# Gated mix of attention and a state-space convolution: the skip term as a lag-0 tap, five-chunk master blocks without negated copies, and zero-weight filler matmuls

## Chip, cores and metric

One NeuronCore of a Trainium2 chip. The metric is the device time of one execution in microseconds (us); the kernel before has a median of 537.9 us over 4 runs. All three parts of the change are in one kernel file, which builds its own instruction order by a planner in Python before anything runs.

## What is computed

x is 2048 x 448 (bf16). Two branches read it and a gate mixes them:

```python
g = sigmoid((x * gate_w).sum(-1, keepdims=True))
a = attention(x)          # 16 heads of 28, one shared k and v, softmax over 2048 keys, then @ wo
b = conv(x, K) + x * Dskip
out = g * a + (1 - g) * b
```

K is a causal kernel of 2048 lags for each of the 448 channels: `K[d, l] = Re sum_n C[d,n] * dB[d,n] * exp(l * dt[d] * A[d,n])` with 256 complex modes n. The reference convolves by FFT; the kernel does it by matmuls with a Toeplitz matrix.

## The kernel before, in words

**Order of work.** Every operation is recorded by `Prog.op` with an engine, a planned duration, the keys that it reads and writes, and a priority `pr` (lower goes first). `Prog.schedule` (L116) then goes through the operations as a list scheduler: of all that are ready, the one with the earliest planned start, then the lowest `pr`, goes next on its engine. It adds 107 ns (`SWITCH`) when the tiling mode of PE changes (`mode`: full, r32, c32, c64). The result is one fixed order per engine, and `emit` (L210) writes it out with semaphore waits. Each engine runs its list in order, so what stands behind a waiting instruction waits too.

**Attention.** 16 groups (4 blocks of 512 queries, 4 groups of 4 heads), each of 16 key tiles x 4 heads: 1024 score tiles of 128 keys x 512 queries. `qk` (L967) makes 3 or 2 of them at a time in one half of psS (two times three banks), as row-tiled matmuls (r32, 29 rows). ACT takes exp of 3 or 2 tiles in one instruction (L977) into a ring of 10 tiles. `pv` (L985) multiplies 4 tiles of one key tile by v with four column-tiled matmuls (c32) and accumulates in the bank psB over 16 key tiles. Then DVE copies the bank out (L933), and the division by the sums goes through small DMAs (L944). `outp` (L877, L883) multiplies by wo and adds the gated result into O (SBUF, all 2048 x 448 outputs). The last group has its own ending (`norm_last`, L899 to L920). `qproj` (L676 to L685) makes the queries of a group two groups ahead in bank psX.

**Convolution.** 28 chunks of 16 channels. Powers of the modes are built from "masters": `masters(b)` squares the complex step ten times (L717, L720, L723), for a block of 4 chunks at once, and writes each level's real part, imaginary part (L727) and negated imaginary part (L730) to mbf. mbf has two halves, used by alternate blocks. `tables(c)` starts from the seeds (L746) and doubles the table five times per chunk: product with the real part (L759), product with the imaginary part into tmp (L762), sum with swapped halves (L767); two more products make the last level (L776, L778). `kgen(c)` multiplies tables on PE (L792) to the 2048 lags of the chunk's kernel; DVE rounds them to kstg (L804, L807) and a DMA puts them into the scratch KP in HBM. `conv(c)`, two chunks later in the program, loads Toeplitz tiles of 1 MB (`tload`, ring of 4), multiplies them by the stored x (U) with four column-tiled matmuls each (L853), multiplies by 1 - g on DVE (L861), transposes on PE (L831) and adds into O (L838). A chunk's L838 touches rows of all four query blocks.

**The skip term.** At the end `skip` (L452) loads x and Dskip again into xT, which is free by then, and DVE does x * (1 - g) * Dskip (L462) and O + that (L465) for each of 16 row tiles, at `pr` 90. `store` then writes each of the four query blocks of O (two on SP's queue, two on ACT's), once all additions to it are done.

**Banks.** psX is shared by qproj, kgen, the transposes and outp under a lock; one bank of psS is shared by kernel preparation and conv.

Of the kernel before, what the change touches and what calls it, by code (L numbers as in the profile page):

```python
# [48 lines left out]
class Op:  # L49
    __slots__ = ("i", "eng", "fn", "ns", "lat", "deps", "pr", "lock", "unlock", "slot", "ndma",  # L50
                 "count", "vc", "end", "comm", "slack", "mode")


class Prog:
# [3 lines left out]
    SWITCH = 107.0  # L58

# [8 lines left out]
    def op(self, eng, fn, ns, rd=(), wr=(), pr=0, lat=60, lock=None, unlock=None, comm=(), slack=None, mode="full"):  # L68
# [5 lines left out]
        o.comm, o.mode = comm, mode  # L74
# [41 lines left out]
    def schedule(self):  # L116
# [18 lines left out]
        pemode = None  # L135
        done = 0
        while done < n:
# [37 lines left out]
            if o.slot is not None:  # L175
                free[e] = r + 450.0 * o.ndma
                s = max(r, dmafree)
                dmafree = s + o.ns
                end = dmafree + self.DMA_NS
            else:  # L180
                ns = o.ns
                if e == "pe":
                    if o.mode != pemode:
                        ns += self.SWITCH
                    pemode = o.mode
                free[e] = r + ns
                end = free[e] + o.lat
# [22 lines left out]
    def emit(self, block):  # L210
# [61 lines left out]
        for e in ENG:  # L272
# [3 lines left out]
            def body(x, e=e):  # L276
                for o, waits in lists[e]:
                    for s, v in waits.items():
# [17 lines left out]
class Kernel:  # L296
# [10 lines left out]
    def build(self):  # L307
        nc = self.nc
        with self.es:
            self.pg = Prog(nc, self.es)  # L310
            self.alloc()
# [13 lines left out]
    def alloc(self):  # L325
# [32 lines left out]
        sizes = [4] * 7  # L358
# [3 lines left out]
        self.AO = [0, 4, 128, 132, 256, 384]  # L362
        self.BO = [448 + 128 * k for k in range(6)]
        self.MC = 448 + 5 * 128 + 64
# [11 lines left out]
        self.zero = sb("zero", 2, BF)  # L376
# [5 lines left out]
    def consts(self):  # L382
# [11 lines left out]
        pg.op("dve", lambda e: e.memset(V(self.kstg, 0, 256), 0.0), 100, wr=[("kst", 0)])  # L394
        ms(self.Wk, NT * P, 0.0, "Wk")
# [15 lines left out]
    def loads(self):  # L411
# [32 lines left out]
        pg.op("dve", lambda e: e.tensor_copy(self.Wv.v(0, DT, 28, [[32, 4]]), self.smallb.v(0, DT, 0, [[1, 4]])), 80, rd=["smb"], wr=["Wv"])  # L444
        w = ins["A_wo"]
# [5 lines left out]

    def skip(self):  # L452
        pg, ins = self.pg, self.ins
        tab = self.xT
        keys = [("xT", hf, j) for hf in range(4) for j in range(2)]
        pg.dma([(tab.v(0, P, 0, [[D, 16], [1, D]]), dram(ins["A_x"], 0, [[D, P], [P * D, 16], [1, D]])),
                (tab.v(0, P, 16 * D, [[1, D]]), dram(ins["B_Dskip"], 0, [[0, P], [1, D]]))],
               (2176, 896), "xs", wr=["xs"] + keys, pr=4)
        for i in range(16):
            tv = tab.v(0, P, D * i, [[1, D]])  # L460
            ov = self.O.v(0, P, D * i, [[1, D]])
            pg.op("dve", lambda e, tv=tv, i=i: e.scalar_tensor_tensor(tv, tv, self.gtok.v(0, P, 16 + i, [[1, 1]]),  # L462
                                                                      tab.v(0, P, 16 * D, [[1, D]]), ALU.mult, ALU.mult),
                  el(D), rd=["gt", "xs"], wr=[("xg", i)], pr=90)
            pg.op("dve", lambda e, tv=tv, ov=ov: e.tensor_tensor(ov, ov, tv, ALU.add),  # L465
                  el(D, 1.92), rd=[("xg", i)], comm=[("O", i // 4)], pr=90)
# [221 lines left out]
    def masters(self, b):  # L688
# [5 lines left out]
        A0 = lambda lv: mo + (BC * (self.AO[lv] // 128 * 128) + self.AO[lv] % 128)  # L694
        pr = 51.5 + c0 if b else 1.4
# [12 lines left out]
        for k in range(11):  # L708
            ks = "sz" if k == 0 else ("ms", k % 2)
            lv, w8 = (k, 16) if k < 5 else (5, 8) if k == 5 else (k - 6, 16)  # L710
            ro, io = A0(lv), mo + BC * self.BO[lv]
            sp_, sn_ = io + 4, io
            if k > 5:
                ro, sp_, sn_ = ro + 8, io + 8, io + 12
            lk = ("mb", b % 2, k)
            if k:
# [10 lines left out]
            pg.op("dve", lambda e, k=k, ro=ro, sp_=sp_, w8=w8: e.tensor_copy(  # L727
                mbf.v(0, P, ro, [[sp_ - ro, 2], [w8, 8 * BC], [1, 4]]), src_both(k)),
                el(2 * BW, 1.92), rd=kk, wr=[lk], pr=pr)
            pg.op("dve", lambda e, k=k, sn_=sn_, w8=w8: e.tensor_scalar(  # L730
                mbf.v(0, P, sn_, [[w8, 8 * BC], [1, 4]]), src(k, 1), -1.0, None, ALU.mult),
                el(BW, 1.92), rd=kk, wr=[(lk, 1)], pr=pr)

    def tables(self, c):
# [14 lines left out]
        for lv in range(5):  # L749
            w = 1 << lv  # L750
            ra = mo + BC * (self.AO[lv] // 128 * 128) + self.AO[lv] % 128 + 128 * ci
            rb = mo + BC * self.BO[lv] + 128 * ci
            mk = [("mb", b % 2, lv), (("mb", b % 2, lv), 1), ("mb", b % 2, lv + 6), (("mb", b % 2, lv + 6), 1)]
            rk = [("tab", s, l) for l in range(lv + 1)]
# [6 lines left out]
                el(n, 1.92), rd=rk + mk, wr=[("tab", s, lv + 1)], pr=pr)  # L761
            pg.op("dve", lambda e, a=src, rb=rb, w=w: e.tensor_tensor(  # L762
                tmp.v(0, P, so, [[4 * w, 32], [1, 4 * w]]), a,
                mbf.v(0, P, rb, [[4, 32], [0, w], [1, 4]]), ALU.mult),
                el(n, 1.92), rd=rk + mk, wr=[("tmp", s)], pr=pr)
            t2 = tmp.v(0, P, so + 4 * w, [[8 * w, 16], [-4 * w, 2], [1, 4 * w]])
            pg.op("dve", lambda e, d=dst, t=t2: e.tensor_tensor(d, d, t, ALU.add), el(n, 1.92),  # L767
                  rd=[("tmp", s), ("tab", s, lv + 1)], wr=[("tab", s, lv + 1)], pr=pr)
        ra = mo + BC * self.AO[5] + 64 * ci
# [323 lines left out]
```

## Time and profile before

| | |
|---|---|
| median of 4 runs | 537.9 us (537.64 to 542.41) |
| the profiled execution, its own time | 537.64 us |
| its span in the trace | 535.9 us |
| mean granted TensorE clock | 0.928 |
| exp on ACT (L977), 410 instructions | 470.5 us busy |
| L759, L762, L767 on DVE, 140 each | 78.5, 78.5, 78.4 us busy |
| DMA | 138.16 MB, mean 258 GB/s |

The span runs from the first to the last instruction in the trace. "L977" is line 977 of the kernel before. "out<-in" names the tiles. A group's mean is the time of one instruction; neighbours on an engine overlap a little, so the busy time of a group is less than count times mean. "a <- b" in the waits says that a started when b had finished. PEld are the weight loads of PE. In the clock row each digit is a tenth of the full TensorE clock, for one of 40 equal slices of the span.

### The profile page before, as it was taken

To read this page: it belongs to the slowest core of one execution; us is meant where nothing else is said; L and a number is where in the kernel's file an instruction comes from. 1 tells how busy PE (TensorE), PEld (TensorE's weight loads), DVE (VectorE), ACT (ScalarE), POOL (GpSimd) and SP (SyncE) were. 2 spreads that over 40 slices of the span, in tenths; PEclk is the share of its full clock that TensorE was granted. 3 is DMA by queue.
4 is the path that set the end of the run, shared out by engine and by line. 5 is a ranking of instruction groups with operands and counts; after the bars stand their busy time and mean duration, and the time that the engine had idled before them with its cause. 6 is when DMAs were issued, how large, how long until landed. Compare 5 with 4: busy or idle time off the path is not lost.

```text
span 535.9 us, 18403 instructions
## 1 busy us (share of the span) xinstructions
PE 478.6 (89%) x8214; PEld 243.8 (45%) x8229; DVE 483.4 (90%) x1168; ACT 487.2 (91%) x428; POOL 4.9 (1%) x17
## 2 busy tenths in 40 slices
PE   6768877998999899999999989999999998998893
PEld 5421122454545344554555435544555543554452
DVE  3978899899999999999999999999999999999023
ACT  3598989999999999999999999999999999999960
POOL 3000000000000000000000000000000000000000
PEclk9855566899999999999999999999999999999997
DMA  9724526588888777878988896878877896799954
GB/s 234 156 66 121 154 87 260 165 299 331 284 320 293 262 275 223 278 261 334 313 317 307 286 325 226 279 242 296 323 273 263 315 368 240 198 359 305 347 187 137
DMA packets 42266, 138.16 MB, mean 258 GB/s; under 512 B 8168, under 2 KB 24476, under 8 KB 27852
## 3 DMA queue, kind: packets, MB, share of 16 engines
q1 hardware_dynamic: 40396, 135.71, 74.2%
q10 hardware_dynamic: 1792, 1.29, 0.9%
q8 instruction: 64, 1.05, 0.8%
q14 instruction: 14, 0.11, 0.1%
HBM read 133.01 MB, written 3.85 MB: 255 GB/s over the span
## 4 chain that ended last, share of the span: by engine, by line
PE 40%; DVE 29%; ACT 27%; DMA 1%; issue 1%; DVEq 0%
ACT expT L977 26%; PE psS L967 11%; PE psS L853 10%; PE psB L985 7%; PE psX L792 5%; DVE tab L759 4%; DVE tmp L762 4%; DVE tab L767 4%; DVE tab L776 2%; PE psX L676 2%; DVE msq L717 2%; DVE tab L778 1%; DVE cst L861 1%; PE psS L504 1%; DVE mbf L727 1%; PE psX L877 1%
## 5 line engine op out<-in xcount | busy, mean ns | idle before, releaser
L977 ACT ACTIVATE expT<-psS 128x1536 bf16<-128x1536 f32 (+1 forms) x410 | 470.5, 1257 | 17.0 <-PE psB L985 11.7
L967 PE MATMUL psS<-qT,kT 29*128 29x512 bf16 x1024 | 169.8, 410 | 33.3 <-ACT expT L977 29.2
L853 PE MATMUL psS<-T,U 128*32 128x128 bf16 (+7 forms) x3584 | 157.2, 303 | 1.5 <-issue 1.0
L853 PEld LDWEIGHTS psS<-T,U 128*32 128x32 bf16 (+7 forms) x3584 | 113.7, 152 | 33.2 <-issue 26.9
L985 PE MATMUL psB<-expT,vaug 128*32 128x512 bf16 x1024 | 108.2, 414 | 1.5 <-ACT gtok L643 1.4
L967 PEld LDWEIGHTS psS<-qT,kT 29*128 29x128 bf16 x1024 | 39.6, 92 | 125.4 <-ACT expT L977 95.3
L762 DVE TENSOR_TENSOR tmp<-tab,mbf 128x2048 bf16<-128x2048 bf16 (+4 forms) x140 | 78.5, 567 | 0.0
L759 DVE TENSOR_TENSOR tab<-tab,mbf 128x2048 bf16<-128x2048 bf16 (+4 forms) x140 | 78.5, 567 | 0.0
L767 DVE TENSOR_TENSOR tab<-tab,tmp 128x2048 bf16<-128x2048 bf16 (+4 forms) x140 | 78.4, 568 | 0.0
L985 PEld LDWEIGHTS psB<-expT,vaug 128*32 128x32 bf16 x1024 | 26.6, 94 | 63.8 <-issue 60.4
L792 PE MATMUL psX<-tab 128*32 128x96 bf16 x1792 | 54.4, 268 | 0.8 <-issue 0.8
L792 PEld LDWEIGHTS psX<-tab 128*32 128x32 bf16 x1792 | 40.7, 116 | 13.6 <-issue 8.0
L776 DVE TENSOR_TENSOR tab<-tab,mbf 128x2048 bf16<-128x2048 bf16 x28 | 34.2, 1220 | 0.0
L778 DVE TENSOR_TENSOR tab<-tab,mbf 128x2048 bf16<-128x2048 bf16 x28 | 34.1, 1216 | 0.0
L861 DVE TENSOR_TENSOR cst<-psS,omq 128x512 bf16<-128x512 f32 x28 | 19.1, 682 | 14.9 <-PE psS L853 14.7
L717 DVE TENSOR_TENSOR msq<-mst 128x256 f32<-128x256 f32 x63 | 26.4, 419 | 0.0
L676 PE MATMUL psX<-xT,Wq 112*128 112x512 bf16 x64 | 21.8, 438 | 0.3 <-DVE O L838 0.2
L727 DVE CAST mbf<-mst 128x256 bf16<-128x256 f32 x70 | 20.4, 291 | 0.1
L720 DVE TENSOR_TENSOR mst<-msq 128x128 f32<-128x128 f32 x70 | 20.0, 286 | 0.0
L723 DVE SCALAR_TENSOR_TENSOR mst<-mst 128x128 f32<-128x128 f32 x63 | 18.0, 286 | 0.0
L730 DVE TENSOR_SCALAR mbf<-mst 128x128 bf16<-128x128 f32 x70 | 15.5, 221 | 0.0
L804 DVE TENSOR_REDUCE kstg<-psX 128x128 bf16<-128x256 f32 x28 | 11.8, 422 | 3.8 <-PE psX L792 3.7
(112 smaller groups left out, 252.2 us busy)
## 6 DMA issues: line engine op xcount, KB each, us to landing
T<-KP_scratch SPq DMA_DIRECT2D x112, 1024.0 KB, 7.9
rdenB<-R_scratch SPq DMA_DIRECT2D x60, 64.0 KB, 3.8
U<-in_A_x_dram SPq DMA_DIRECT2D x3, 896.0 KB, 5.4
tab<-in_A_x_dram SPq DMA_DIRECT2D x4, 448.0 KB, 7.0
O<-Z_scratch SPq DMA_DIRECT2D x1, 1792.0 KB, 13.4
KP_scratch<-kstg SPq DMA_DIRECT2D x28, 64.0 KB
xT<-in_A_x_dram SPq DMA_DIRECT2D x1, 1792.0 KB, 9.7
U<-Z_scratch SPq DMA_DIRECT2D x1, 896.0 KB, 7.9
```

The lines of the kernel that those rows point to most:

```text
L676: pg.op("pe", lambda e, T=T: e.matmul(px, self.Wq.v(0, DT, T * 512 + g * 128, [[1, 128]]), self.xT.v(0, DT, T * S + 512 * qc, [[1, 512]]), ...
L717: pg.op("dve", lambda e, k=k: e.tensor_tensor(msq.v(0, P, 0, [[1, 2 * BW]]) if k > 1 else msq.v(0, P, 0, [[BW, 2], [1, BW]]), src_both(k - ...
L759: pg.op("dve", lambda e, d=dst, a=src, ra=ra, w=w: e.tensor_tensor(d, a, mbf.v(0, P, ra, [[8, 16], [0, 2 * w], [1, 4]]), ALU.mult), el(n, ...
L762: pg.op("dve", lambda e, a=src, rb=rb, w=w: e.tensor_tensor(tmp.v(0, P, so, [[4 * w, 32], [1, 4 * w]]), a, mbf.v(0, P, rb, [[4, 32], [0, w ...
L767: pg.op("dve", lambda e, d=dst, t=t2: e.tensor_tensor(d, d, t, ALU.add), el(n, 1.92), rd=[("tmp", s), ("tab", s, lv + 1)], wr=[("tab", s, ...
L776: pg.op("dve", lambda e: e.tensor_tensor(ua, src, mbf.v(0, P, ra, [[8, 8], [0, 64], [1, 4]]), ALU.mult), el(2048, 1.92), rd=rk + mk, wr=[( ...
L778: pg.op("dve", lambda e: e.tensor_tensor(ub, src, mbf.v(0, P, rb, [[4, 16], [0, 32], [1, 4]]), ALU.mult), el(2048, 1.92), rd=rk + mk, wr=[ ...
L792: r = e.matmul(self.psX.v(32 * g, 32, 96 * jj, [[1, 96]]), tab.v(0, P, o + 768, [[4, 32]]), tab.v(0, P, o, [[256, 3], [4, 32]]), start=(co ...
L853: r = e.matmul(ps.v(32 * j, 33 - m, po + 128 * k, [[1, 128]]), self.U.v(0, P, (m - 1) * D + 4 * gi + j, [[D, 33 - m]]), self.T.v(0, P, s * ...
L967: r = e.matmul(self.psS.v(0, P, 1536 * s + 512 * k, [[1, 512]]), kT.v(32 * h, DH + 1, 128 * kt, [[1, 128]]), qT.v(32 * h, DH + 1, 512 * qs ...
L977: pg.op("act", lambda e: e.activation(expT.v(0, P, 512 * (i0 % 10), [[1, n]]), self.psS.v(0, P, 1536 * s, [[1, n]]), AF.Exp, scale=SQ), 75 ...
L985: r = e.matmul(self.psB.v(32 * h, 32, 0, [[1, 512]]), vaug.v(0, P, 32 * kt, [[1, 32]]), expT.v(0, P, 512 * ((4 * st + h) % 10), [[1, 512]] ...
```

## The change

- **Skip term.** `skip` is gone. Dskip is loaded once into row 31 of a zeroed tile dsk. At the end of each `kgen` chunk, four small matmuls with the identity add it into the column of lag 0 in psX. So x * Dskip is part of the convolution. For this the start flag of the L792 group is set once per chunk instead of once per column range.
- **Masters.** Block sizes go from seven of 4 chunks to one of 3 and five of 5. Real and imaginary parts lie side by side in mbf, and the negated copy is written for level 5 only. In `tables`, the product with the imaginary part reads that layout, and the sum becomes two instructions of half the length, an addition and a subtraction. The masters' `pr` now rises level by level through the block before, where it was one value for all levels. The planned duration of the cast goes from 202 to 342 ns at its new width.
- **Fillers.** While the P.V bank is open (from the first to the last key tile of a group), the planner looks at PE's planned idle time before each PE operation. If it is long enough, and the planned use of the array over the last 3413 ns is below 46%, it puts fillers in front: four column-tiled matmuls of zero weights by 256 columns of kT, added into psB. They have no wait of their own; they stand ahead of the operation's waits. The planned time of the operations themselves is not moved by them.

```diff
+    FILL_NS, FILL_MAC, FILL_WIN, FILL_RATE, FILL_GAP = 107.0, 256.0, 3413.0, 0.46 * 2.4, 130.0
...
+        o.mac = mac if mac is not None else min(ns, 2000.0) * 1.2 if eng == "pe" else 0.0
...
                 if e == "pe":
+                    t = free[e]
+                    while isopen:
+                        cost = self.FILL_NS + (self.SWITCH if pemode != "c32" else 0.0)
+                        if r - t < cost + self.FILL_GAP:
+                            break
+                        past = [x for x in past if x[0] > t - self.FILL_WIN]
+                        if sum(x[1] for x in past) >= self.FILL_RATE * self.FILL_WIN:
+                            nxt = min(x[0] for x in past) + self.FILL_WIN + 1.0
+                            if r - nxt < cost + self.FILL_GAP:
+                                break
+                            t = nxt
+                            continue
+                        o.pre += 1
+                        t += cost
+                        past.append((t, self.FILL_MAC))
+                        pemode = "c32"
+                    past.append((r, o.mac))
+                    if o.open is not None:
+                        isopen = o.open
                     if o.mode != pemode:
                         ns += self.SWITCH
...
                 for o, waits in lists[e]:
+                    if o.pre:
+                        self.filler(x, o.pre)
...
-        sizes = [4] * 7
+        sizes = [3, 5, 5, 5, 5, 5]
...
+        ms(self.dsk, D, 0.0, "dsk")
+        ms(self.zw, 32, 0.0, "zw")
...
+        pg.dma([(self.dsk.v(31, 1, 0, [[1, D]]), dram(ins["B_Dskip"], 0, [[D, 1], [1, D]]))], (1, 896), "dsk", wr=["dsk"])
...
+            pr = 52.5 + self.blocks[b - 1][0] + (self.blocks[b - 1][1] - 1) * (k + 1) / 11.0 if b else 1.4
...
-            pg.op("dve", lambda e, k=k, ro=ro, sp_=sp_, w8=w8: e.tensor_copy(
-                mbf.v(0, P, ro, [[sp_ - ro, 2], [w8, 8 * BC], [1, 4]]), src_both(k)),
-                el(2 * BW, 1.92), rd=kk, wr=[lk], pr=pr)
-            pg.op("dve", lambda e, k=k, sn_=sn_, w8=w8: e.tensor_scalar(
-                mbf.v(0, P, sn_, [[w8, 8 * BC], [1, 4]]), src(k, 1), -1.0, None, ALU.mult),
-                el(BW, 1.92), rd=kk, wr=[(lk, 1)], pr=pr)
+            pg.op("dve", lambda e, k=k, ro=ro, st=st, dc=dc: e.tensor_copy(
+                mbf.v(0, P, ro, [[dc, 2], [st, 8 * BC], [1, 4]]), src_both(k)),
+                el(2 * BW, 1.17), rd=kk, wr=[lk], pr=pr)
+            if k == 5:
+                pg.op("dve", lambda e, k=k, ro=ro: e.tensor_scalar(
+                    mbf.v(0, P, ro + BC * 64, [[8, 8 * BC], [1, 4]]), src(k, 1), -1.0, None, ALU.mult),
+                    el(BW, 0.87), rd=kk, wr=[(lk, 1)], pr=pr)
...
-            t2 = tmp.v(0, P, so + 4 * w, [[8 * w, 16], [-4 * w, 2], [1, 4 * w]])
-            pg.op("dve", lambda e, d=dst, t=t2: e.tensor_tensor(d, d, t, ALU.add), el(n, 1.92),
-                  rd=[("tmp", s), ("tab", s, lv + 1)], wr=[("tab", s, lv + 1)], pr=pr)
+            for k, (o0, ds, t0, ts, op) in enumerate(((0, 384, 4 * w, 4 * w, ALU.add), (128, 128, 0, 12 * w, ALU.subtract))):
+                d = tab.v(0, P, do_ + o0, [[1024, 8], [ds, 2], [1, 4 * w]])
+                t2 = tmp.v(0, P, so + t0, [[16 * w, 8], [ts, 2], [1, 4 * w]])
+                pg.op("dve", lambda e, d=d, t=t2, op=op: e.tensor_tensor(d, d, t, op), el(n // 2, 1.92),
+                      rd=[("tmp", s), ("tab", s, lv + 1)], wr=[("ts", s, lv + 1, k)], pr=pr)
...
-                            start=(comp == 0 and half == 0), stop=(comp == 1 and half == 1),
+                            start=(jj == 0 and comp == 0 and half == 0), stop=False,
                             tile_position=(0, 32 * g), skip_group_check=True)
+                if jj == 3 and comp == 1:
+                    for g in range(4):
+                        r = e.matmul(self.psX.v(32 * g, 32, 95, [[96, 4]]), self.ident.v(0, P, 0, [[1, 32]]),
+                                     self.dsk.v(0, P, 16 * c + 4 * g, [[1, 4]]), start=False, stop=True,
+                                     tile_position=(0, 32 * g), skip_group_check=True)
...
+    def filler(self, e, n):
+        for _ in range(n):
+            for h in range(4):
+                e.matmul(self.psB.v(32 * h, 32, 0, [[1, 256]]), self.zw.v(0, P, 0, [[1, 32]]), self.kT.v(0, P, 0, [[1, 256]]),
+                         start=False, stop=False, tile_position=(0, 32 * h), skip_group_check=True)
...
-        self.skip()
         for tt in range(4):
             self.outp(3, tt, tt)
```

## The prediction

> **What bounds the kernel now.** I read the page first, then busy time by stage, waits, groups by form, and the timeline of the end. The page:
>
> ```profile
> span 535.9 us, 18403 instructions
> ...
> PE 478.6 (89%) x8214; PEld 243.8 (45%) x8229; DVE 483.4 (90%) x1168; ACT 487.2 (91%) x428; POOL 4.9 (1%) x17
> ...
> PEclk9855566899999999999999999999999999999997
> ```
>
> Three engines near 90% say little; the stages say more. Busy time by stage (columns: stage, its length, PE, PEld, DVE, ACT, POOL busy, granted clock, DMA share, GB/s):
>
> ```profile
> 40.00:107.00 67.00, 56.79 (x603) 18.27 (x604) 61.14 (x158) 60.28 (x53) 0.00 (x0) 0.63 0.48 157
> 107.00:490.00 383.00, 361.64 (x6835) 191.01 (x6850) 380.03 (x923) 373.38 (x326) 0.63 (x2) 1.00 0.83 290
> 490.00:518.50 28.50, 24.94 (x448) 12.82 (x440) 7.99 (x18) 28.26 (x26) 0.00 (x0) 1.00 0.88 309
> ```
>
> ACT idles 6.7 us (10%) in the first stage, where TensorE has 0.63 of its clock, 9.6 us (2.5%) in the second, 0.2 in the third. DVE is full (99%) to 490 and then nearly empty, while ACT runs exp to 518. So from 24 us, the first exp, ACT sets the pace, and DVE's end at about 491 is no longer what ACT waits for. ACT's waits (total us, times, longest):
>
> ```profile
> ACT expT L977 <- PE psB L985: 11.7, 27, 1.1
> ACT expT L977 <- PE psS L967: 4.0, 8, 0.7
> ```
>
> ACT waits for PE alone, 15.7 us in the main loop. Then 17.6 us of end follow the last exp (518.3). In the timeline (start, us):
>
> ```profile
> 516.79 0.82 PEld L853 LDWEIGHTS psS<-T,U 128*28 128x28 bf16 x24
> ...
> 523.21 1.07 PE L853 MATMUL psS<-T,U 128*30 128x128 bf16 x28
> ...
> 526.66 0.68 DVE L861 TENSOR_TENSOR cst<-psS,omq 128x512 bf16<-128x512 f32 x1
> 527.26 0.68 DVE L883 SCALAR_TENSOR_TENSOR O<-psS,gtok,O 128x448 bf16<-128x448 f32 x1
> ...
> 528.04 0.42 DVE L838 TENSOR_TENSOR O<-O,psX 128x256 bf16<-128x256 bf16 x1
> 528.49 0.96 SPq L106 DMA_DIRECT2D out_dram<-O  x2
> 528.49 1.05 ACTq L106 DMA_DIRECT2D out_dram<-O  x2
> ```
>
> The convolution of chunk 27 (L853, L861, L838) lies between the last attention steps. L838 adds into every row of O, so all four stores wait for it and leave together at 528.5; they take 7.4 us to the end of the span. That is the place where DVE's lateness is on the path.
>
> [...] in 53.6 to 67 us the clock is 0.50, and the 28 score tiles and as many P.V tiles of 128 full-array columns each fill 28 x 256 / (13.4 x 2400) = 22% of the array; from 107 to 134, with 224 conv matmuls (32 each) and 104 of L792 (24 each), 39%, and the clock is 1.00. [...] starts of 2048-element bf16 products lie 1.13 us apart, 2048/1.92 + 61 ns. [...] LDWEIGHTS shows 0.44 us ahead of a mode change at half clock (61.09 us), 0.23 at full (250.09). [...]
>
> **Part by part, DVE.** I use start-to-start times, since neighbours overlap by some 90 ns.
> - Skip removed: L462 0.60 + L465 0.30, x16 = 14.4 us. They lie at 445 to 494 at the lowest priority; about 3.9 us of them after 490. So 10.5 before. Some filled waits between dependent products of chunk 27 (480 to 489); call 2.5 of it free cover. Real relief before the last kernel rows: 8.
> - Masters. One level now: L717 0.33, L723 0.21, L720 0.20, L727 0.20, L730 0.13 = 1.08 us; 7 blocks x (10 x 1.08 + 0.34) = 78. After: no L730 but for level 5. At 5 chunks the widths grow by a quarter: 0.40 + 0.24 + 0.24 + 0.23 = 1.11; five blocks x (11.1 + 0.4) = 57.5. The block of 3: 0.78 a level, 8.1. Sum 65.6; saved 12.3. The new cast writes its real and imaginary runs side by side; if that costs a half of its rate, 61 casts x 0.1 = 6 us come back. I take none: L727 writes runs of four either way.
> - Table sums: L767 becomes two of half length, 140 more instructions x 61 ns = +8.6.
> - Two memsets of zero, about 0.3 us: covered by the 3.6 us in which DVE waits for the first transposes (7.3 us). Without cover 0.3.
>
> Net about -18 us of DVE in all, about -12 before the last kernel rows (8 + 12.3 - 8.6): they move from 491 to about 479. ACT doesn't wait for that; it is worth what the end makes of it.
>
> **Queues.** SP: one DMA of 896 bytes for Dskip more, issued ahead of Wo and the pads, some 0.5 us of SP's queue (a T load takes 0.51 to issue); Wo is first needed past the fourth of 16 groups, after 140 us. Two DMAs of the skip, 1.9 MB, fall away: at the stage's 290 GB/s 6.6 us of transfer, hidden before.
>
> **The end.** Chunk 27 now closes 528.5 - 518.3 = 10.2 us behind the last exp; the T loads (1 MB each, DMA share 0.9 to 1.0 from 470 to 512) follow the kernel rows. Twelve us earlier, its L838 falls at about 516. Then (a) the tail loses what the convolution puts into it: L861 delays the fourth L883 by 0.5, so that O's last writer would end at 527.4 instead of L838's 528.5 (-1.0), and the chunk's matmuls stand ahead of L915 and L877 for some 0.5 (estimate from 521.8 to 524.2 us): -1.5. (b) Three of four stores leave before. A store of 448 KB alone: about 1 us before bytes move (528.5 to about 529.4) plus 0.46 MB at 275 GB/s (1.7) plus landing; estimate 3.8 us instead of 7.4: -3.6. (c) Without conv the PE may fall to half clock during the last 8 us: +0.3. Sum -4.8. If chunk 27 stays late, none of it: that is the other bound.
>
> **Fillers.** PE has none now. The planner puts groups of four column-tiled matmuls of 256 before an instruction when its own gap exceeds 237 ns (344 after a mode change) and the last 3413 ns hold under 46% of the array. In the early stage the density is 22%, and a group adds 256 columns: (0.46 - 0.22) x 2400 / 256 = 2.2 a us would close it, if gaps allow. At full clock one is 107 ns. Gain: ACT's idle share in 40 to 107 goes from 10% towards the 2.5% of the later stage, 67 x 0.075 = 5 us; I subtract 1 for the first us in which fillers run at half clock ahead of scores, and 0.5 for the stalls of about 1 us that are in the order (42.0, 73.3). Gain 3.5; bounds: 0 to 5, and a loss in the third rival. From 107 on the clock is 1.00 already, so fillers there can only cost. The density is about 0.4 there and plan gaps are short: estimate 0.1 a us, 40 in all. [...] I take one in ten of full weight: +1.2. All of them: +12.
>
> **TensorE, rest.** Four matmuls of 4 columns per chunk at the end of L792: at its 30 ns spacing 0.12 us x 28 = 3.4 us of PE, covered by PE's waits for ACT (95 us on L967's weight loads); a third uncovered, +1. Spreading the masters' priorities removes bursts (5 or 6 of L717 in one 10 us slice at 110, 170, 360, 420) with which ACT gaps are not clearly lined up: 0.
>
> **Sum** against the profiled execution: 535.9 - 4.8 - 3.5 + 1.2 + 1.0 = 529.8 span. That run took 537.64, 1.74 more than its span, and the median of the four is 537.9: so 531.5, -1.2%.
>
> **Rivals.**
> 1. Likeliest (0.50): as summed, 531.5; own range 528.5 to 534.5.
> 2. Swallowed (0.27): PE, 94% busy in 107 to 490, takes fillers, extra matmuls and a denser kernel supply badly. At 20 ns more for each of 326 exps, +6.5 instead of +2.2: 535.8; if instead chunk 27 stays late, 531.5 + 4.8 = 536.3. For it: PE's order is fixed and exp waits for PE only. Against: weight loads wait 95 us for ACT.
> 3. Slower (0.08): fillers do not raise the clock. At half clock one exp interval (67/53 = 1.26 us) holds a score group and 0.63 of a P.V group at 0.54 each = 0.88; the projections bring it near 1.0. A filler is 0.21, so from 1.3 fillers an exp PE becomes the bound. At 2.2, +0.2 x 53 = 11 us instead of -3.5: 546. [...]
> 4. More (0.15): the order under lighter DVE also closes a third of the 9.6 us that ACT idles after 107, (3.2) and the early stage gives 5: 531.5 - 3.2 - 1.5 = 526.8. For it: DVE holds up PE at L831 (7.9 us of waits on L861).
>
> **Range and chances.** Rivals 1, 2 and 4 span 525 to 537.5, leaving out the third and edges: 525 to 538. The likeliest's own is 528.5 to 534.5. About 1% is what a measurement tells from no change. Faster by over 1% (under 532.5): 0.75 of case 1, all of 4, 0.53 in all; slower 0.08; the rest within.
>
> **What would show it.** Right: PEclk near 1.0 from about 45 us; ACT idle in 40 to 107 near 3 us; last L838 before the last exp; three stores issued before the last; L804 of chunk 27 near 479; L767 x280, L730 x6. Wrong: clock still 0.5 at 60 us; ACT idle in the middle above 15 us; four stores together; a cast mean well above 330 ns.

## The result, and the profile after

The changed kernel takes 537.3 us (median of 35 runs) against 539.1 for the kernel before (56 runs of the same sittings): a ratio of 0.996, 95% interval 0.995 to 0.998. That is within 1%; the forecast was 531.5. It lies inside the range, near its upper end, but only about 0.3 of the promised gain is there. Here and in the table below, a ratio leaves out executions over 1.5% above the fastest of their kernel, while a median takes in all.

The execution that was profiled first had a span of 540.3 us, above the median, so I show a second one. The page of the changed kernel:

```profile
span 537.4 us, 20092 instructions
...
PE 496.0 (92%) x9069; PEld 260.6 (48%) x9069; DVE 469.9 (87%) x1166; ACT 487.1 (91%) x428; POOL 4.8 (1%) x17
...
PEclk9765989998999999999999999999999999999998
```

PE has 17 us more, DVE 14 less, and the fifth to eighth digits of the clock (54 to 107 us) have risen. By stage (stage, its length, PE, PEld, DVE, ACT, POOL busy, granted clock, DMA share, GB/s):

```profile
40.00:107.00 67.00, 60.52 (x940) 24.93 (x942) 62.90 (x191) 62.68 (x56) 0.00 (x0) 0.89 0.56 179
107.00:490.00 383.00, 371.37 (x7214) 198.51 (x7214) 368.83 (x896) 371.51 (x324) 0.53 (x2) 1.00 0.81 281
490.00:518.50 28.50, 27.00 (x521) 14.32 (x520) 3.68 (x7) 27.98 (x25) 0.00 (x0) 1.00 0.87 300
```

ACT idles 4.3 us in the first stage (6.7 before) and 11.5 in the second (9.6 before). Its waits (total us, times, longest) have moved in part from P.V to the scores:

```profile
ACT expT L999 <- PE psB L1007: 7.9, 18, 1.1
ACT expT L999 <- PE psS L989: 7.8, 13, 1.4
```

The timeline of the end, in which the last exp is over at 518.4:

```profile
513.57 0.69 DVE L877 TENSOR_TENSOR cst<-psS,omq 128x512 bf16<-128x512 f32 x1 [11.37 <-PE psS L869]
515.15 0.42 DVE L854 TENSOR_TENSOR O<-O,psX 128x256 bf16<-128x256 bf16 x1 [0.89 <-PE psX L847]
...
528.25 0.68 DVE L877 TENSOR_TENSOR cst<-psS,omq 128x512 bf16<-128x512 f32 x1
...
529.48 0.42 DVE L854 TENSOR_TENSOR O<-O,psX 128x256 bf16<-128x256 bf16 x1 [0.54 <-PE psX L847]
529.92 0.96 SPq L108 DMA_DIRECT2D out_dram<-O  x2
529.93 1.05 ACTq L108 DMA_DIRECT2D out_dram<-O  x2
```

Chunk 27 is where it was: L854 (the former L838) comes last, and four stores leave together. From the last exp to the end of the span it is 19.0 us, against 17.6 before.

The two profiled executions differ by +1.5 us of span: -2.4 ACT idle in 40 to 107, +1.9 in 107 to 490, +1.4 at the end, +0.6 elsewhere. The medians differ by -1.8, because the profiled execution of before (537.64) is 1.5 quicker than its median and this one (539.24) 1.9 slower than its own.

### The profile page after: what moved, and what is told of

Same layout as the page of the kernel before. It is cut to its first block, busy times and chain, and to the rows that moved or that the text cites. A ratio compares the mean times of both kernels' runs of the same rounds, so it can differ in the third digit from the quotient of the medians.

```text
span 540.3 us, 20077 instructions
## 1 busy us (share of the span) xinstructions
PE 496.3 (92%) x9054; PEld 261.4 (48%) x9069; DVE 470.0 (87%) x1166; ACT 488.1 (90%) x428; POOL 4.8 (1%) x17
## 4 chain that ended last, share of the span: by engine, by line
PE 51%; ACT 38%; DVE 7%; issue 2%; DMA 1%
ACT expT L999 36%; PE psS L989 14%; PE psS L869 13%; PE psB L1007 9%; PE psX L803 5%; PE psB L905 2%; PE psX L687 2%; PE psS L515 1%; PE psX L893 1%; DVE tab L778 1%; DVE tab L768 1%; DVE tmp L771 1%; DMA tab<-in_A_x_dram 1%; PE psX L847 1%; PE psS L893 1%
## 5 line engine op out<-in xcount | busy, mean ns | idle before, releaser
L869 PE MATMUL psS<-T,U 128*32 128x128 bf16 (+7 forms) x3584 | 160.8, 302 | 5.5 <-issue 4.5
L778 DVE TENSOR_TENSOR tab<-tab,tmp 128x256 bf16<-128x256 bf16 (+2 forms) x280 | 89.7, 360 | 0.5
L768 DVE TENSOR_TENSOR tab<-tab,mbf 128x128 bf16<-128x128 bf16 (+4 forms) x140 | 78.8, 566 | 0.5
L771 DVE TENSOR_TENSOR tmp<-tab,mbf 128x128 bf16<-128x128 bf16 (+4 forms) x140 | 78.6, 564 | 0.0
L905 PE MATMUL psB<-kT,zw 128*32 128x256 bf16 x728 | 39.0, 305 | 0.0
L726 DVE TENSOR_TENSOR msq<-mst 128x320 f32<-128x320 f32 (+1 forms) x54 | 24.9, 462 | 0.0
L905 PEld LDWEIGHTS psB<-kT,zw 128*32 128x32 bf16 x728 | 19.4, 107 | 9.7 <-issue 7.4
L736 DVE CAST mbf<-mst 128x320 bf16<-128x320 f32 (+1 forms) x60 | 18.7, 311 | 0.0
L729 DVE TENSOR_TENSOR mst<-msq 128x160 f32<-128x160 f32 (+1 forms) x60 | 18.4, 307 | 0.0
L732 DVE SCALAR_TENSOR_TENSOR mst<-mst 128x160 f32<-128x160 f32 (+1 forms) x54 | 16.6, 307 | 0.0
```

Source lines behind the costliest of these rows:

```text
L768: pg.op("dve", lambda e, d=dst, a=src, ra=ra, w=w: e.tensor_tensor(d, a, mbf.v(0, P, ra, [[8, 16], [0, 2 * w], [1, 4]]), ALU.mult), el(n, ...
L771: pg.op("dve", lambda e, a=src, ra=ra, w=w: e.tensor_tensor(tmp.v(0, P, so, [[4 * w, 32], [1, 4 * w]]), a, mbf.v(0, P, ra + 4, [[8, 16], [ ...
L778: pg.op("dve", lambda e, d=d, t=t2, op=op: e.tensor_tensor(d, d, t, op), el(n // 2, 1.92), rd=[("tmp", s), ("tab", s, lv + 1)], wr=[("ts", ...
L869: r = e.matmul(ps.v(32 * j, 33 - m, po + 128 * k, [[1, 128]]), self.U.v(0, P, (m - 1) * D + 4 * gi + j, [[D, 33 - m]]), self.T.v(0, P, s * ...
L905: e.matmul(self.psB.v(32 * h, 32, 0, [[1, 256]]), self.zw.v(0, P, 0, [[1, 32]]), self.kT.v(0, P, 0, [[1, 256]]), start=False, stop=False, ...
```

## The experiments

Ratios are against runs of before in the same sitting. The last column is the plain ratio of the two medians over all executions. Where the two differ by 0.4% or more, the kernel's executions spread widely, and neither is relied on alone.

| kernel | median, us | ratio to before, 95% | ratio of medians |
|---|---|---|---|
| changed kernel, again | 537.3 | 0.995 (0.993 to 0.998) | 0.997 |
| fillers_only | 541.2 | 1.000 (0.997 to 1.002) | 1.004 |
| masters_only | 537.7 | 0.996 (0.994 to 0.999) | 0.997 |
| no_fillers / again | 534.4 / 533.1 | 0.991 (0.989 to 0.994) / 0.990 (0.988 to 0.992) | 0.991 / 0.989 |
| no_fillers_shifted / again | 537.7 / 538.7 | 0.998 (0.996 to 1.001) / 1.002 (0.999 to 1.004) | 0.998 / 1.000 |
| before_shifted | 539.7 | 1.002 (1.000 to 1.005) | 1.002 |
| shifted | 535.8 | 0.995 (0.993 to 0.996) | 0.994 |
| early_fillers | 536.2 | 0.994 (0.992 to 0.996) | 0.995 |
| early_shifted | 533.3 | 0.989 (0.985 to 0.993) | 0.990 |
| early_dense / again | 531.8 / 535.0 | 0.989 (0.984 to 0.993) / 0.988 (0.982 to 0.993) | 0.987 / 0.993 |
| dense_shifted | 532.1 | 0.987 (0.984 to 0.990) | 0.987 |
| no_chunk27 (work left out) | 534.0 | 0.985 (0.978 to 0.992) | 0.991 |
| half_sums (work left out) | 533.5 | 0.989 (0.986 to 0.993) | 0.990 |

**The parts.** after_again is the changed kernel unchanged. fillers_only puts the fillers alone into the kernel before, masters_only the master blocks and table sums alone (skip back at the end, no fillers); no_fillers takes the fillers out:

```diff
-                    while isopen:
+                    while False:
```

> The changed kernel once more, for a second trace. Theory A (the fillers' gain and loss cancel, and the lighter DVE moves nothing because the Toeplitz loads hold chunk 27): ACT idle in 40 to 107 us again near 6.5 us, last kernel rows again near 490 us, four stores together. Theory B (the first trace was an unlucky execution, 4.8 us above the median, and a usual one shows what was predicted): ACT idle there near 3.5 us, last kernel rows near 480 us, three stores early. Time near 0.996 of the kernel before either way.

> The kernel before with the fillers alone. Theory A: 0.995 to 1.0 of before; ACT idle below 2 us in 80 to 107 but above 4 us in 40 to 60. Theory B (fillers give the 2.3 us net that was predicted, and the rest of the change costs as much): 0.993 to 0.996.

> The kernel before with the new masters and table sums alone; skip stays at the end, no fillers. Theory A: no more than 0.5% slower than before; the sums' 8.6 us eat most of the masters' 12.3, so DVE's busy time falls by 3 to 4 us and the last kernel rows stay within 4 us of 490. If the skip's removal had been what frees DVE, this one would show the rows some 8 us later than the kernel without fillers.

> The changed kernel without the fillers: skip as a tap and the new masters. Theory A: within 0.3% of before, since DVE's 17 us come off an engine that nobody on the path waits for; DVE idle after 107 us grows by what DVE saves; last kernel rows at 488 to 492 us. Theory B: DVE parts cost time, 1.002 to 1.006. If the prediction's own step held, 0.991 with rows near 479 us.

after_again fits neither theory whole: ACT idles 4.3 us in 40 to 107 and the last kernel rows come at 486.6, between the two, while the stores leave together as in theory A. Fillers alone give nothing. Masters alone give 0.4%, with the last kernel rows at 494.5, later than the 490.0 of before. With the skip as a tap as well (no_fillers) it is 0.9%, and the rows are at 484.0: the time is that of "the prediction's own step" in its expectation, the rows are not. So it looked as if the fillers took half of the gain back. That reading fell later (see the shifted kernels).

**The end.** no_chunk27 leaves out the convolution of chunk 27 and the DMA of its kernel rows. half_sums leaves out the second of each two table sums (some 43 us of DVE's work) and, like no_fillers, has no fillers:

```diff
+        if c == NCH - 1:
+            return
...
-            if 0 <= cc < NCH:
+            if 0 <= cc < NCH - 1:
```

```diff
-            for k, (o0, ds, t0, ts, op) in enumerate(((0, 384, 4 * w, 4 * w, ALU.add), (128, 128, 0, 12 * w, ALU.subtract))):
+            for k, (o0, ds, t0, ts, op) in enumerate(((0, 384, 4 * w, 4 * w, ALU.add),)):
```

> The changed kernel without the convolution of chunk 27 (its 16 channels lack their convolution; its kernel rows are made and not written out). Theory A (the prediction's tail step is right in size, only chunk 27 didn't move): from the last exp to the end of the span 13.5 to 15 us instead of 19, three stores issued before the last, time 0.985 to 0.989 of before. Rival (the end is set by the last group's normalization and one store's landing whatever the others do): tail 17.5 us or more, 0.993 or slower.

> The changed kernel without fillers and with the second of each two table sums left out (the kernels K are wrong). DVE has some 43 us less to do. Theory A (chunk 27 is held by the chain of Toeplitz loads and by the planned order behind it): last kernel rows some 40 us earlier, near 443 us, but the last addition to O only about 12 us earlier, near 512; with chunk 27 out of the tail 0.981 to 0.985 of before. Rival (DVE's pace holds everything, also ACT): last addition near 485 us and ACT's idle time from 107 to 490 below 4 us; 0.975 or less.

The stores of no_chunk27, in its timeline:

```profile
517.14 0.95 SPq L108 DMA_DIRECT2D out_dram<-O  x2
517.14 0.47 ACTq L108 DMA_DIRECT2D out_dram<-O  x1
529.37 0.39 ACTq L108 DMA_DIRECT2D out_dram<-O  x1
```

Three leave 12 us ahead of the last, and from the last exp (520.5) to the end of the span (532.6) it is 12.1 us. With half_sums it is 12.2. So the forecast's -4.8 for a chunk 27 out of the way was, if anything, small: -5.5 against before, -6.9 against the changed kernel. It just isn't reached in a full kernel. In half_sums the last kernel rows are written at 447.6, over 30 us earlier than in any full kernel and 36 earlier than in no_fillers, and L854 comes at 517.8: only seven us earlier than the 524.8 of no_fillers. That is 1.6 us ahead of the last exp, so here the tail is short; the time, 0.989, is still not the 0.981 to 0.985 of theory A, as the exps are later than in no_fillers (below).

**Fillers and the early clock.** early_fillers keeps fillers only before 110 us of the plan (77 groups of 182); early_dense also plans no gap for the real work, and at up to 0.9 of the array, before 60 us (114 groups):

```diff
-                    while isopen:
+                    while isopen and t < 110000.0:
...
-                        if r - t < cost + self.FILL_GAP:
+                        if r - t < cost + (0.0 if t < 60000.0 else self.FILL_GAP):
...
-                        if sum(x[1] for x in past) >= self.FILL_RATE * self.FILL_WIN:
+                        if sum(x[1] for x in past) >= (0.9 * 2.4 if t < 60000.0 else self.FILL_RATE) * self.FILL_WIN:
```

> The changed kernel with fillers only where the plan is before 110 us: 77 groups instead of 182. Theory A (later fillers cost about 3 us in standing PE and buy nothing, the early ones about break even): 0.990 to 0.993, near the kernel without fillers. Rival (the loss comes from the early stage, where fillers at half clock delay scores): 0.995 to 0.997, as with all of them.

> The changed kernel with fillers only before 110 us of the plan, and before 60 us without a gap kept for the real work and at a rate of 0.9 in place of 0.4 (114 fillers planned in place of 77). Theory G (the fillers pay only in executions where the clock rises at once, in 40-60 us; more activity makes it rise in nearly all): executions lie closer together than those with 77 fillers, and 0.986 to 0.991 of before. Rival H (at half clock each filler delays the exps, and a denser supply only delays more): 0.996 to 1.004.

> Fillers before 110 us, dense before 60 us, once more: 0.986 to 0.991 of before if the first six executions were ordinary, 0.992 to 0.996 if they were fortunate. In its profile, if the clock rises in 40-60 us, the exp run is 5 to 6 us ahead of before at 108 us; if only later, 1 to 3.

early_dense, measured twice, and its shifted form dense_shifted are 1.1 to 1.3% below before by the ratios (0.7 to 1.3% by the medians), and so beat both kernels. They are not told apart from no_fillers in its own place (0.990 and 0.991). The two profiles of early_dense show one way in which executions of one kernel differ. The stage 40 to 60 us, first in early_dense, then in dense_again, the same kernel:

```profile
40.00:60.00 20.00, 19.04 (x358) 8.93 (x363) 19.77 (x77) 19.88 (x18) 0.00 (x0) 1.00 0.50 137
```

```profile
40.00:60.00 20.00, 20.00 (x268) 7.31 (x267) 17.02 (x72) 16.24 (x15) 0.00 (x0) 0.70 0.50 125
```

In the first the clock is 1.00 from 40 us and ACT is busy 19.9 of 20 us. In the second it is 0.50 until about 52 us; PE is busy all the time with fillers at half speed, and ACT runs three exps fewer. At the end of the 60th exp (108 us in before) the first is 5.5 us ahead of before, the second 0.5, less than the 1 to 3 that dense_again's expectation gave for a late rise; the spans are 528.0 and 534.5. The same split is in the others: ahead by 6.0 in early_fillers and 5.9 in shifted (clock 1.00 in 40 to 60 in both), by 2.6 in after_again (0.71), by 2.6 in early_shifted (0.50 until 60 us), by 0.1 in the first profile of the changed kernel (0.50 until 64 us). Without fillers it is 1.9 to 2.1 in three profiles and 0.3 in a fourth. Over 36 executions of the changed kernel, each 0.01 of mean clock goes with 1.9 us of span (correlation -0.79); in 51 executions of before, which has no fillers, it is 2.3 us (-0.72), so this alone says nothing about fillers. The rise comes at different times in equal programs: in the two profiled executions of the changed kernel at 51.8 and at 64.4 us. What decides it stays open.

So by 108 us fillers are worth about 4 us if the clock rises at once. If it doesn't, the profiles lie from 0.7 us better to 1.9 worse than most without fillers, which is about as much as those differ among themselves. Dense ones don't make it rise always. Behind 110 us these kernels have almost no fillers, so that none can cost anything there. Theory G of the expectation, a rise in nearly all executions and a small spread, is wrong in that part: they spread from 528 to 538. By the medians the second six (0.993) make the first six the fortunate set of dense_again's expectation, by the ratios (0.988) an ordinary one. early_fillers itself, at 0.994, falls between its theory and its rival.

**Places in the instruction list.** The profiles show standstills of PE in the main loop with no wait, marked "issue". shifted, no_fillers_shifted, before_shifted, early_shifted and dense_shifted put 40 small matmuls (80 instructions, with their weight loads) at PE's first idle, so that all later ones move on by 80 places:

```diff
+        def pad(e):
+            for _ in range(40):
+                r = e.matmul(self.psB.v(0, 32, 0, [[1, 32]]), self.ident.v(0, P, 0, [[1, 32]]), self.ident.v(0, P, 0, [[1, 32]]),
+                             start=True, stop=True, tile_position=(0, 0), skip_group_check=True)
+            return r
+        pg.op("pe", pad, 900, rd=["id"], wr=[("b", 6)], pr=-9)
```

> The changed kernel with 40 small matmuls more in PE's first idle time, which shift every later PE instruction by 80 places. In two traces of the changed kernel PE stands still for 0.6 to 1.6 us at the same four matmuls, whose places in PE's list are all 0.67 to 0.70 of the way through a run of 256. Theory F (the standstill belongs to the place in the list, in blocks of 256 instructions): the standstills move to other matmuls, again near 0.7 of 256; their number may change and the time with it by up to 3 us. Rival (it belongs to what those matmuls do or to fillers ahead of them): the same four matmuls stand still, 0.995 of before.

> Kernel without fillers, with 40 small matmuls added at PE's first idle, so that every later PE instruction stands 80 places further on in its list. Theory F (the standstills of 0.6 to 1.9 us without a visible wait belong to places in PE's list): the one standstill of the kernel without fillers (0.96 us at 389.01) goes from its matmul, others may turn up; since that kernel had only one, there is little to win: 0.988 to 0.994 of before. Rival P (the 40 matmuls help by themselves, because they keep TensorE active early and raise its clock): the clock in 40-60 us rises to 1.00 and the time falls to 0.985 or lower.

> The kernel without fillers once more. Theory K (the time belongs to the kernel's own list, whichever chip execution): 0.990 to 0.993 of before, executions within 1 us of one another. Rival L (an execution's luck, so the first six were a fortunate set): 0.995 to 0.999, spread over 4 us or more like the shifted one.

> The kernel without fillers and with the 40 small matmuls once more; its profiled execution was its quickest of 22, so this one is likely to be an ordinary one. Theory F: an ordinary execution (span 535 to 537) shows standstills of 0.6 us or more that the quick one (one, 0.84) did not show, about 3 us together. Rival C: it shows none, and the time is lost in 40-107 us, where the clock is low.

> The kernel before with the same 40 small matmuls at PE's first idle, nothing else changed. The profile of before shows no standstill of 0.6 us or more. Theory F: the shift can only bring some; the time is 0.999 to 1.005 of before. Rival P (the 40 matmuls raise the early clock or help otherwise by themselves): 0.995 or lower.

> The changed kernel with fillers only before 110 us of the plan (77 groups) and the 40 small matmuls. Theory F with G: the two standstills of the version without the small matmuls (1.89 at 120.58, 0.80 at 244.80) leave their matmuls; if no long ones take their place, 0.988 to 0.992 of before; each new one costs back about its length. Rival (standstills cost nothing, only the clock counts): as the version without the small matmuls, 0.992 to 0.996, whatever the standstills.

> Fillers before 110 us, dense before 60 us, and the 40 small matmuls. If the gain of the dense version belongs to its clock: 0.985 to 0.992 of before again. If it belongs to a lucky place of its instructions in PE's list: 0.993 to 0.998.

The first expectations held in part: in shifted the standstills moved, as theory F says, but at 0.995 the time is that of the rival too. no_fillers in its own position is 0.99 in both measurements, with executions within 0.6 us (standard deviation); shifted by 80 places it is 0.998 and 1.002, with a deviation of 2. The forecast for no_fillers_shifted was a miss; the 40 matmuls themselves are not the reason, since before_shifted is only 0.2% up. The profiled execution of no_fillers_shifted was the quickest of its 22 (span 532.1); that of no_fillers_shifted_again is the third slowest of its 14 (539.5). The chain of work that ended last in no_fillers_shifted_again, in two windows (start us, us, what):

```profile
248.72 0.49 PE psS L876 x12
249.21 1.28 issue
250.50 0.32 PE psS L876 x2
```

```profile
391.05 0.66 PE psS L876 x14
391.71 1.43 issue
393.14 0.70 PE psS L876 x15
```

Inside a run of equal convolution matmuls, and with no wait in the trace, PE stands still. From the 160th to the 180th exp this execution falls back behind before by 2.2 us (no_fillers_shifted by 1.2, with a standstill of 0.84 at that place), from the 300th to the 320th by 3.1 (no_fillers_shifted by 0.3). These two stretches make up 3.8 of the 7.4 us between the two executions; another 1.8 lies before 108 us. The standstills themselves are only 1.9 us longer than in no_fillers_shifted. The rest fits the clock, which is halved just after the second standstill, for 6.8 us (busy time by stage, before and after the standstill):

```profile
385.00:391.70 6.70, 6.51 (x147) 3.73 (x146) 6.49 (x21) 6.70 (x7) 0.00 (x0) 1.00 0.92 315
393.40:400.20 6.80, 6.80 (x91) 2.62 (x84) 5.99 (x11) 4.98 (x5) 0.00 (x0) 0.50 0.78 276
```

ACT loses 1.8 of these 6.8 us. A halved clock follows within 2 us in six of the eleven standstills of 1.2 us or more in all traces, after_again's first one among them; ten such drops between 107 and 520 us come without a standstill of 0.6 us. That the standstill brings the drop is thus likely and not shown.

In the page of the changed kernel the instructions have a queue of their own (packets, MB, share):

```profile
q8 instruction: 71, 1.16, 0.9%
```

71 packets of 16384 bytes, for PE's 18138 matmuls and weight loads, which is one for 255; the page of before has 64 for 16443, one for 257. That a packet carries 256 of PE's instructions is an estimate from these counts. I counted PE's instructions in the traces, its semaphore instructions among them, up to each standstill and each packet:

```
kernel                      standstill from, us   instructions so far = n x 256 + rest   packet in flight, us
after_again                 121.71 (1.59)          3009 = 11 x 256 + 193                 120.95 to 122.05
after_again                 463.04 (0.90)         15809 = 61 x 256 + 193                 461.67 to 462.64
after_again                 488.52 (1.23)         16833 = 65 x 256 + 193                 487.17 to 488.23
early_fillers               118.69 (1.89)          3009 = 11 x 256 + 193                 118.01 to 119.09
no_fillers_shifted_again    249.22 (1.28)          6849 = 26 x 256 + 193                 248.00 to 249.10
no_fillers_shifted_again    391.71 (1.43)         11969 = 46 x 256 + 193                 390.71 to 391.60
shifted                     259.83 (1.40)          8385 = 32 x 256 + 193                 258.92 to 259.88
shifted                     267.48 (1.61)          8641 = 33 x 256 + 193                 266.59 to 267.70
```

These are long ones of four traces. In the 10 traces with standstills of 0.6 us or more in which every weight load has its matmul, all of them lie at rest 193. In the other four 15 or 16 matmul records are missing, and the rest comes out at 178 to 189; with one matmul taken for each weight load it is 192 or 193 there too. Each standstill of the table begins within half a us of a packet's landing and ends 1.2 to 1.5 us after it, as if PE had used up its instructions; that it waits for the packet is read from these times alone. The packet in flight is number n - 1, counted from 0, so that PE stops 256 + 193 = 449 places on from (n - 1) x 256. Why it is 449 is not shown. In shifted the four standstills of the changed kernel are gone from their matmuls and two new ones stand at the same place of other runs. So in these kernels the place in the list decides where PE can stand still, and the 80 instructions ahead moved all of these places.

Whether a packet comes late varies. On the scale on which PE stops at 449, a packet set out with PE at 177 to 221 where the DMA engines were less than half busy in the 6 us before, and at about 270 to 313 where they were over 80% busy (medians of each profile; only 1 to 7 packets of a profile are of the first kind). That the Toeplitz loads hold it up is likely from this, but no run without them was made, so it is argued and not shown.

before and early_shifted show no standstill of 0.6 us or more, before_shifted one (0.64), early_dense one (0.76) and none in its second profile, no_fillers one (0.96) and none in its second; the first profile of the changed kernel has four, 4.1 us together, after_again four, 4.4, and half_sums six, 5.5. dense_shifted has two (0.79, 0.98) and still 0.987: its gain outlasts the shift, so it isn't a lucky place alone. Its clock is 0.99 in 40 to 60 us.

With both positions counted, no_fillers is 0.990 to 1.002 and the changed kernel 0.995 to 0.996. Whether the fillers as planned gain or lose can't be said beyond that; the place in the list is worth as much. Why no_fillers takes more time 80 places on is read from one execution, the one above, and only in part.

## Why the prediction was wrong, by its own steps

**"The end": the step that failed.** The kernel rows "move from 491 to about 479", and "Twelve us earlier, its L838 falls at about 516": from this came the term of -4.8. Two things are wrong in it.

First, the rows moved less. before writes them at 490.0, no_fillers at 484.0, after_again at 486.6, masters_only (skip still there) at 494.5. DVE's work ahead of them did fall nearly as told: up to the last rows it is busy 468.8 us in before and 457.9 in the other two, -10.9 of the -12. But its idle time up to there grew from 21.2 us to 26.1 and 28.7, which the forecast had put at nothing. Only a small part is a wrong price: the two sums cost +9.6 from start to start and not +8.6, since the fixed part of an instruction is 68 ns in before (1135 ns apart at 2048 elements, 135 at 128) where 61 was taken. Masters did what was said: 77.7 us from start to start in before, 65.4 now, against 78 and 65.6. The new cast takes 0.24 us from start to start, told 0.23, and its mean (the last but one number below, in ns) stays under the 330 that would have been a sign of an error.

```profile
L736 DVE CAST mbf<-mst 128x320 bf16<-128x320 f32 x50 | 16.1, 322 | 0.0
```

Second, and this decides, earlier rows don't bring chunk 27 forward. early_shifted has them at 480.1, about where the forecast wanted them, since the whole execution is ahead; its timeline:

```profile
480.09 0.42 DVE L827 TENSOR_REDUCE kstg<-psX 128x128 bf16<-128x256 f32 x1 [2.75 <-PE psX L817]
...
508.54 0.69 DVE L884 TENSOR_TENSOR cst<-psS,omq 128x512 bf16<-128x512 f32 x1 [11.88 <-PE psS L876]
...
522.06 0.42 DVE L861 TENSOR_TENSOR O<-O,psX 128x256 bf16<-128x256 bf16 x1 [0.54 <-PE psX L854]
```

The chunk's result is 42 us behind its rows, and again behind the last exp (511.3). In every full kernel L838 or its successor comes 9.7 to 11.9 us behind the last exp, whatever the rows do. What holds it is the chunk ahead. The profile of before already had it:

```profile
497.38 0.69 DVE L861 TENSOR_TENSOR cst<-psS,omq 128x512 bf16<-128x512 f32 x1 [2.44 <-PE psS L853]
...
511.29 0.69 DVE L861 TENSOR_TENSOR cst<-psS,omq 128x512 bf16<-128x512 f32 x1 [12.26 <-PE psS L853]
512.75 0.42 DVE L838 TENSOR_TENSOR O<-O,psX 128x256 bf16<-128x256 bf16 x1 [0.77 <-PE psX L831]
```

Chunks 25 to 27 leave PE at 497, 511 and 527, one in 14 to 15 us, while DVE waits 12 us for chunk 26. SP's queue in before (start, us), where the last four loads of Toeplitz tiles, those of chunk 27, are the last two rows:

```profile
491.70 0.56 SPq L106 DMA_DIRECT2D KP_scratch<-kstg  x1
492.30 5.59 SPq L106 DMA_DIRECT2D T<-KP_scratch  x3
...
500.91 4.06 SPq L106 DMA_DIRECT2D T<-KP_scratch  x2
...
508.74 3.06 SPq L106 DMA_DIRECT2D T<-KP_scratch  x2
```

Its longest waits in 478 to 515 us (total us, times, longest):

```profile
SPq L106 <- PE psS L967: 23.5, 8, 6.8
```

The first load of chunk 27 starts 9 us after its rows have gone out: the loads wait for PE to release tiles, and for kernel rows there is no wait in that list. Earlier in the main loop SP's queue does wait for rows (L807: 24.0 us in six waits), but PE waits for a Toeplitz load only once, 0.3 us; so late rows didn't hold PE up. It runs the chunks between the scores in the fixed order of the plan. With chunk 26 at 512.75 and one chunk in 14 us, chunk 27 could not be at 516. No run moved chunk 27 alone forward in PE's list, so what holds it is read from these waits, while half_sums shows that the rows don't. So the term was 0 and not -4.8; measured is +1.4, and what adds these 1.4 stays open. From -4.8 to +1.4 makes 6.2 of the 7.6 us by which the profiled execution misses its forecast span (537.4 against 529.8).

**Fillers, early: -3.5.** ACT's idle in 40 to 107 fell by 2.4 in after_again, not at all in the first profile of the changed kernel, by 4.7 and 5.4 in early_fillers and early_dense; in no_fillers it fell by 1.0 without any filler. Where the clock rises at once, the step holds (clock 0.97 in 40 to 107 in early_fillers and early_dense, 0.63 in before). The planner's bound for the density was my own setting, and no run varies it alone. The text had one state and "the first us in which fillers run at half clock"; it is all of 40 to 60 us in some executions, and in these the third rival's picture, PE full of fillers at half clock, is the right one for that long (early_shifted: clock 0.50, PE busy 20.00 of 20 us, ACT 15.4). The sign to look for, PEclk near 1.0 from 45 us, came in part: 0.53 in 48 to 52, 1.00 from 52 in after_again.

**Fillers, later, and the small matmuls: +1.2 and +1.0.** ACT's idle in 107 to 490 grew by 1.9, near the 2.2. The term took one filler in ten to delay a score by 0.3 us, which was an estimate; such delays are at most part of it: 109 of the 182 groups run after 107 us and not 40, while four standstills of PE (4.4 us) and a halved clock for 3.4 us after the first of them were not in the list of costs at all. Without fillers the stage has 8.0 and 6.8 us, less than before, but 12.2 in no_fillers_shifted_again. The small matmuls, told at 0.12 us for four, take 0.13 us from the first of four to PE's next matmul (median); what of it is uncovered was not measured.

**DVE -18.** From start to start, as it was told, the parts come to -14.4 (skip), -12.2 (masters) and +9.6 (sums): -17.0, so this was nearly right. DVE's busy time, a different measure, falls from 483.4 to 469.9: -13.5. As the forecast said, ACT doesn't wait for it; half_sums, with another 38 us off DVE in 107 to 490, has its last exp at 519.4 and so later than no_fillers (514.3). It has six standstills, though, against one; without the 4.5 us that these are longer, the two are about level. So DVE's end doesn't make the gain without fillers; it is the idle time of ACT (8.0 against 9.6 and 5.7 against 6.7) and an earlier start by about 1 us. What shortens that idle time is not shown, and by the medians the gain doesn't outlast a shift by 80 places.

**Chances.** The second rival, swallowed by late fillers or by a chunk 27 that stays late, 536.3, is what came, by the second of its two ways. That 537.3 still lies in the range of 525 to 538 owes to the range's width; the likeliest case's own range is missed.

## What to carry to other kernels

Before you let a late item move forward because its input comes earlier, look where the item ahead of it in the same pipeline ends and at its pace: the earliest possible time is that plus one step. Put fillers for the clock where the clock is low; here those after 110 us, where it was 1.00 already, bought nothing that could be measured (0.996 with them, 0.994 without). Judge them over many executions, since one profile shows one state of the clock (1.00 and 0.70 in 40 to 60 us in two of the same kernel). A difference of 1% can come from where the instructions lie in PE's list: here a shift by 80 places took no_fillers from 0.990 and 0.991 to 0.998 and 1.002. Shift the list once before you believe it.

## What the runs showed of the hardware

- Fillers of zero weights went with a higher clock in most profiles: in 40 to 60 us it was 0.50 in before, no_fillers, no_fillers_again and no_fillers_shifted_again; with fillers it was 0.99 to 1.00 in early_dense, early_fillers, shifted and dense_shifted, 0.71 and 0.70 in after_again and dense_again, and 0.50 in early_shifted and in the first profile of the changed kernel.
- PE stood still for 0.6 to 1.9 us as a packet of the instruction queue (16384 bytes) landed, in the ten complete traces with such standstills at place 193 of a run of 256 by my count; each of the two profiles of the changed kernel, with 71 packets, showed four such places.
- The clock was halved in the middle of a stage in which PE is over 90% busy: for 6.8 us (393.4 to 400.2) in no_fillers_shifted_again, right after a standstill of 1.43 us, and for 3.4 us (185.6 to 189.0) in before, which shows no standstill.
- Matmuls of 512 columns start 215 to 227 ns apart at clock 1.00 (L676 in before); the lower end is 2.4 columns a ns, the rate that the prediction reckons with. A group of four fillers of 256 columns starts 109 ns after the group ahead of it at clock 1.00, and 213 ns at 0.50 (first profile of the changed kernel, medians).
- The table sums of before (L767, VectorE, bf16 in SBUF) take 135, 202, 335, 602 and 1135 ns from start to start at 128, 256, 512, 1024 and 2048 elements: 68 ns besides the 0.52 ns of each element.
- The four matmuls of 4 columns (L810) start 4 to 5 ns apart (median), though each shows 0.19 us.
